# Attention in seven key chunks over two pairs at once, its division moved into the w_in stage, and the row sums of two quads in one phase

## The chip, the cores and the metric

The kernel runs on one core of one Trainium2 chip. The metric is the device time of one execution, in microseconds (us). The kernel before takes 799.59 us, the median of three runs (799.35 to 800.0).

## The reference, cut to what matters

Attention over 8 batches of 12 heads, 448 tokens, head size 64, with q and k normalised row by row, and behind it a feed-forward block on the 3584 x 768 result (inner width 1024). All of it is in float32.

```python
q_n, k_n = rmsnorm(q, g_q), rmsnorm(k, g_k)            # x / sqrt(mean(x*x) + 1e-6) * g
scores = q_n @ k_n.T / sqrt(64)
attn = exp(scores - max) ; attn = attn / (sum(attn) + 1e-9)
x = (attn @ v) laid out as (B*S, H*D)                  # 3584 x 768
h = x @ w_in                                           # 768 x 1024
solu = h * softmax(h)
ln = (solu - mean) / sqrt(var + 1e-6) * g_ln
out = ln @ w_out                                       # 1024 x 768
```

## The kernel before, in words

`fast_path` has three stages, one behind the other: attention, the product with w_in (with the activation and the layer norm of each token tile behind it), and the product with w_out. The order of all instructions is written out by hand: `unit(f)` emits one piece of TensorE work and then whatever was put down to be due, `later(n, f)` puts f down for n units later, and `follow(parts, i, f)` emits f right behind part i. Each engine, and each engine's DMA queue, works in the order of emission and waits at an instruction whose inputs are not there.

**Attention.** The work goes by quads, 24 of them, `for m in range(NQ)` (L1432): a quad is four heads, as two pairs a = 2m and b = 2m + 1. q and k are loaded by 8 transfers per quad on SP's queue (`load`, L631), squared on ScalarE (`squares`, L670), summed by row on VectorE (`row_sums`, L676). The two halves of a row's sum lie in neighbouring groups of 32 partitions: GpSimd copies them across in four copies and adds (`fold_sums`, L684). The inverse root is a Ln and an Exp on ScalarE and four small VectorE instructions (`rsqrt_seed` L693, `rsqrt_step` L700); GpSimd multiplies (`normalise`, L709); VectorE transposes in 32 x 32 blocks (`qk_transpose`, L720); ScalarE applies the gain to q (`gain`, L725).

The 448 keys of a pair are cut into three chunks of 128 (`scores`, L810) and a last one of 64, which two pairs share (`scores_last`, L824): seven groups of four 64 x 64 tiles of TensorE in a quad. ScalarE takes the exponential of each group from PSUM, 128 x 896 at a time (`exponentials`, L806). There is no maximum: the scores are bounded by the gains. The product with v is again seven groups of four tiles: `values_last` (L859) and `values_part` (L873) twice, the two parts apart because a row tile has to change its PSUM bank in between (`turn`, L899, a wait through ScalarE). The first scores of the next quad run between the two parts.

The row sums of the exponentials are a product with ones (`sums`, L914), in tiles of 128 rows by 32 columns. It takes four terms: the shared chunk, one chunk of pair b, and for each pair a tile that VectorE has added up (`add`, L842); GpSimd adds the third chunk of pair a to its tile (`add_more`, L853). Each quad has its own phase of these products at its end. Then the sums are turned, inverted and spread to all rows of the output (`inverse`, L936: a VectorE transpose, a reciprocal, four GpSimd copies; `divide`, L952: a VectorE transpose and the multiplication of the PSUM output, 128 x 896), and the result goes to DRAM by two transfers on SP's queue (`store_x`, L961). The next quad's first values wait for `divide`, since there is one output tile in PSUM.

Beside this, w_in is loaded and converted from float64 in 12 steps (`convert_w`, L518: two ScalarE and two VectorE instructions a step), at the quads of `steps_at` (L1376), and GpSimd forms the combinations of its blocks (`combine_in`, L565).

**w_in.** Seven products instead of eight per block of 256 tokens, 14 blocks g. `load_x(g)` (L974) brings x back from DRAM, for g >= 2 on ScalarE's queue. `sizes` (L985) is two ScalarE instructions, `block_sums` (L1005) four GpSimd ones. `products` (L1019) gives seven parts p1 to p7, each six matmul instructions; `in_parts` (L1149) sets their order, for block g: p6, p5, p7, p1 of g + 1, p4, p2 of g + 1, p3. Behind the parts of block g stand `sizes(g + 1)` and the two halves of `block_sums(g + 1)`, and at the fifth of them `load_x(g + 2)`. The activation and the layer norm of each token tile follow by `later` (`ff_max` to `ff_spread`, L1099 to L1147): on VectorE the sum of two partial products (L1053), the product h * exp (L1112), two statistics (L1120), a transpose (L1141). w_out is loaded and converted beside it.

**w_out.** The same scheme on quarter blocks. The change does not touch it.

Of the kernel before, what the change touches and what calls it, by code (L numbers as in the profile page):

```python
# [366 lines left out]
def fast_path(  # L367
# [29 lines left out]
    NB = S // 32  # L397
    NP = H // 2
# [26 lines left out]
    ones = consts.tile([P, 3, 32], FP32, name="ones")  # L425

    w_in = {k: wi.tile([P, HD, DFF // 2], FP32, name=f"w_in{k}") for k in (0, 5, 1, 4, 3, 6, 2)}
    xd = [dram.tile([DM, S], FP32, name=f"xd{b}") for b in range(B)]
    ud = [dram.tile([2, 4, 32, HF * P], FP32, name=f"ud{t}") for t in range(NT)]
# [88 lines left out]
    def convert_w(step, raw):  # L518
# [15 lines left out]
        def low_bits():  # L534
            nc.scalar.activation(low, lo, AF.Relu, scale=-(2.0 ** -29), bias=seven)
            nc.scalar.activation(tmp[:, 1].bitcast(I32), low, AF.Copy, scale=-1.0, bias=7.0)
# [93 lines left out]

    def load(m):  # L631
        qk = loads.tile([P, 2, 2, NB * 32], FP32, tag="qk", name="qk", bufs=4)
        for s, src in enumerate((q, k)):
            rows = heads(src, m).rearrange("(h i) (b t) (x d) -> h x t (i b) d", h=2, t=32, x=2)
            for g in range(4):
                nc.sync.dma_start(  # L636
                    qk[g * 32 : g * 32 + 32, s].rearrange("p i (b d) -> p (i b) d", d=32), rows[g // 2, g % 2]
                )
        for i in range(2):
            st[2 * m + i] = {"qk": qk[:, :, i]}  # L640

    def load_v(m, queue=nc.sync):


        d = quads[m] = {}
        d["v"] = loads.tile([P, 4, NJ, D], FP32, tag="v", name="v", bufs=2)
        queue.dma_start(
            d["v"].rearrange("p h j d -> p h (j d)"),
            heads(v, m)[:, 0 : NJ * P].rearrange("h (p j) d -> p h (j d)", j=NJ),
        )  # L650
        if m % 2 == 0:
            vl = loads.tile([P, 4, D], FP32, tag="vl", name="vl", bufs=2)
            two = heads(v, m, 8)[:, NJ * P : S].rearrange("(h i) p d -> i p h d", i=2)
            for i in range(2):
                nc.sync.dma_start(vl[i * D : (i + 1) * D], two[i])
                lasts[m + i] = vl[:, 2 * i : 2 * i + 2]
        d["vl"] = lasts.pop(m)
# [15 lines left out]

    def row_sums(n):  # L676
        m, i = divmod(n, 2)
        if i == 0:
            norms[m] = {"part": small.tile([P, 2, 2 * NB], FP32, tag="part", name="part", bufs=2)}
# [159 lines left out]
    def on_vector(m):  # L839
        return m >= NQ - 2  # L840
# [911 lines left out]
```

## Time and profile before

| | |
|---|---|
| time, median of 3 runs | 799.59 us |
| span of the profiled execution | 798.0 us |
| attention, from the start to its last row sums | 311.4 us |
| w_in stage | from 311.7 us to about 565 us |
| w_out stage | from there to the end |
| TensorE busy over the span | 99% |
| VectorE, ScalarE, GpSimd busy | 76%, 59%, 66% |

The profiled execution's own time is its span, 798.0 us from the first to the last instruction; the timed runs are 1.6 us above it, which is what lies around the span. A timeline line gives the start, the duration (of a merged run of like instructions, from the first start to the last end), the engine, the line of the kernel, the operation, output<-input with shapes, and in brackets the idle time of the engine before it and what ended that. Each float32 product stands in the profile as two matmul instructions, so a group of four tiles is eight. "PEld" is the weight load, which runs beside the products. A busy TensorE is not a TensorE at its peak.

### The profile page before, as it was taken

The page shows a single profiled execution, that of the slowest core. Times are in us where ns is not written, and L with a number is a line of the kernel's source. Part 1 is how long each engine was busy: PE and PEld are TensorE (multiplying, and loading weights), DVE is VectorE, ACT ScalarE, POOL GpSimd, SP SyncE. Part 2 cuts the span into 40 slices and gives each one's busy share as a digit, 9 for nine tenths or more (in the row PEclk, how much of TensorE's full clock was granted, in tenths as well). Part 3 has the DMA queues.
Part 4 walks back from the last instruction along what each step waited for, and adds up shares of the span by engine and source line. Part 5 has one row for each costly group of instructions (what it writes and reads, how often), then busy time and mean ns, then how long its engine had stood idle before and what let it go on. Part 6 is the DMA issues. An engine that isn't in the chain of part 4 may idle for free.

```text
span 798.0 us, 15285 instructions
## 1 busy us (share of the span) xinstructions
PE 786.3 (99%) x5382; PEld 468.8 (59%) x5382; DVE 608.7 (76%) x1153; ACT 472.5 (59%) x783; POOL 524.2 (66%) x665
## 2 busy tenths in 40 slices
PE   8999999999999999999999999999999999999997
PEld 4344444444444444444444444444799999999996
DVE  6787989989888895587777667776896776866945
ACT  6777988878779763566766544454515455464410
POOL 2666777778877775243466466668787777877861
PEclk9999999999999999999999999999999999999999
DMA  8878799898787742455545445542757547366312
GB/s 166 162 181 166 165 198 187 198 189 164 166 164 175 152 109 74 132 137 147 152 132 145 106 110 143 140 122 53 207 151 235 176 168 262 127 210 229 108 60 84
DMA packets 266913, 122.74 MB, mean 154 GB/s; under 512 B 184012, under 2 KB 251980, under 8 KB 266828
## 3 DMA queue, kind: packets, MB, share of 16 engines
q1 hardware_dynamic: 252988, 111.78, 56.0%
q10 hardware_dynamic: 13840, 9.90, 4.4%
q8 instruction: 44, 0.72, 0.4%
q14 instruction: 41, 0.34, 0.1%
HBM read 84.94 MB, written 36.70 MB: 152 GB/s over the span
## 4 chain that ended last, share of the span: by engine, by line
PE 86%; DVE 5%; SPq 2%; DMA 2%; issue 1%; ACT 1%; POOL 1%; DVEq 0%; ACTq 0%; POOLq 0%
PE A L1252 14%; PE s L818 13%; PE o L882 12%; PE BD L1037 11%; PE A L1037 11%; PE B L1252 7%; PE sm L931 5%; PE C L1037 5%; PE C L1252 3%; PE o L868 2%; PE s L831 2%; SPq L636 1%; DMA ur<-ud 1%; DVE ub L1141 1%; PE o L909 1%
## 5 line engine op out<-in xcount | busy, mean ns | idle before, releaser
L808 ACT ACTIVATE E<-s 128x896 f32<-128x896 f32 x168 | 141.2, 932 | 11.4 <-PE s L818 11.2
L818 PE MATMUL s<-qkT 64*64 64x448 f32 x1152 | 124.2, 544 | 1.4 <-ACT qkT L792 0.6
L882 PE MATMUL o<-E,v 64*64 64x448 f32 x1056 | 107.1, 536 | 0.0
L1126 POOL TENSOR_TENSOR he<-he,mhalf 128x1 f32<-128x1 f32 x28 | 27.3, 975 | 103.3 <-DVE he L1125 102.8
L818 PEld LDWEIGHTS s<-qkT 64*64 64x64 f32 x1152 | 49.8, 163 | 58.3 <-ACT E L808 25.0
L857 POOL TENSOR_TENSOR es<-es,E 128x896 f32<-128x896 f32 x23 | 49.1, 2133 | 49.4 <-DVE es L845 49.4
L1252 PE MATMUL A<-w_out,sums 128*128 128x192 f32 x392 | 80.0, 327 | 1.2 <-DVE u L1266 1.2
L713 POOL TENSOR_TENSOR qkn<-qk,ny 128x896 f32<-128x896 f32 x46 | 77.9, 1713 | 3.7 <-DVE ny L707 1.5
L1252 PE MATMUL B<-w_out,sums 128*128 128x192 f32 x392 | 79.8, 326 | 0.4 <-DVE P L1314 0.4
L1037 PE MATMUL A<-w_in,xg 128*128 128x512 f32 x168 | 74.6, 593 | 0.0
L882 PEld LDWEIGHTS o<-E,v 64*64 64x64 f32 x1056 | 40.2, 133 | 58.3 <-issue 58.1
L1108 ACT ACTIVATE u<-h,hmax 128x1024 f32<-128x1024 f32 x28 | 32.2, 1148 | 66.4 <-DVE hmax L1102 66.4
L1037 PE MATMUL BD<-w_in,xsum 128*128 128x512 f32 x156 | 71.2, 592 | 0.0
L1252 PEld LDWEIGHTS A<-w_out,sums 128*128 128x128 f32 x392 | 66.1, 190 | 2.3 <-issue 1.4
L1252 PEld LDWEIGHTS B<-w_out,sums 128*128 128x128 f32 x392 | 66.2, 190 | 0.8 <-DVE P L1314 0.7
L845 DVE TENSOR_TENSOR es<-E 128x896 f32<-128x896 f32 x48 | 57.2, 1195 | 0.0
L1037 PEld LDWEIGHTS A<-w_in,xg 128*128 128x128 f32 x168 | 31.8, 190 | 40.1 <-issue 39.3
L723 DVE STREAM_TRANSPOSE qkT<-qkn 128x896 f32<-128x896 f32 x46 | 50.9, 1106 | 4.4 <-POOL qkn L713 4.4
L1037 PEld LDWEIGHTS BD<-w_in,xsum 128*128 128x128 f32 x156 | 29.5, 190 | 37.5 <-issue 35.4
L690 POOL COPY ss<-part 32x56 f32<-32x56 f32 x92 | 46.3, 503 | 6.5 <-DVE part L680 2.2
L680 DVE TENSOR_REDUCE part<-sq 128x28 f32<-128x896 f32 x46 | 47.7, 1077 | 0.8 <-ACT sq L672 0.8
L1252 PE MATMUL A<-w_out,s 128*128 128x192 f32 x224 | 45.6, 326 | 0.3 <-ACT u L1264 0.3
(160 smaller groups left out, 1662.6 us busy)
## 6 DMA issues: line engine op xcount, KB each, us to landing
ur<-ud SPq DMA_DIRECT2D x60, 256.0 KB, 4.7
ud<-ub SPq DMA_DIRECT2D x112, 128.0 KB, 2.3
xd<-xo SPq DMA_DIRECT2D x48, 224.0 KB, 3.0
qk<-in_q_dram SPq DMA_DIRECT2D x92, 112.0 KB, 3.1
qk<-in_k_dram SPq DMA_DIRECT2D x92, 112.0 KB, 3.1
v<-in_v_dram SPq DMA_DIRECT2D x24, 384.0 KB, 4.7
out_dram<-P SPq DMA_DIRECT2D x19, 384.0 KB, 3.7
raw<-in_moe_w_in_dram SPq DMA_DIRECT2D x12, 512.0 KB, 5.0
```

Source lines behind the costliest of these rows:

```text
L680: nc.vector.tensor_reduce(norms[m]["part"][:, i], st[n]["sq"], AX, OP.add)
L690: e.tensor_copy(ss[g * 32 : g * 32 + 32], part[o * 32 : o * 32 + 32])
L713: e.tensor_tensor(d["qkn"].rearrange("p (s b) d -> p s b d", s=2), d["qk"].rearrange("p s (b d) -> p s b d", d=32), y.rearrange("p (s b) - ...
L723: nc.vector.transpose(d["qkT"].rearrange("p s t -> p (s t)"), d["qkn"].rearrange("p b d -> p (b d)"))
L808: nc.scalar.activation(d["E", kc], s[:, :, 0:S], AF.Exp)
L818: nc.tensor.matmul(s[c : c + D, h, 0:S], d["qkT"][hh, 1, keys], d["qkT"][hh, 0, :], start=True, stop=True,)
L845: nc.vector.tensor_tensor(d["es"], d["E", 0], d["E", 1], OP.add)
L857: e.tensor_tensor(d["es"], d["es"], d["E", 2], OP.add)
L882: x = nc.tensor.matmul(d["o"][h * D : (h + 1) * D, :], quads[m]["v"][pp, i + 2 * h, kc], d["E", kc][pp, h], start=False, stop=(part == 1 a ...
L931: nc.tensor.matmul(sm[g : g + 32, :], ones[:, w], e[:, h, t * S // 2 : (t + 1) * S // 2], start=(x == 0), stop=(x == len(terms) - 1),)
L1037: nc.tensor.matmul(k[bank], a[:, c], w_in[i][:, c], start=begin and c == 0, stop=c == HD - 1, skip_group_check=not begin,)
L1252: nc.tensor.matmul(k[bank], a[:, c].rearrange("p a i -> p (a i)"), w_out[:, area, i, c], start=begin and c == 0, stop=c == KC - 1, skip_gr ...
```

## The change

- **Chunks.** Both pairs of a quad go side by side through seven chunks of 64 keys (`both_scores`, `both_values`), each one group of four tiles. Keys are taken with a stride of 7. The parts, the turn and the early scores of the next quad are gone. The gain is one instruction for both pairs. v is loaded by two transfers of 64 partitions. Quad 0 keeps its chunks, with its values at its end.
- **Sums.** VectorE adds chunks 0, 1 and 2 into one tile for both pairs, and 3 and 4 into a second; chunks 5 and 6 are terms of their own: four terms. In quads from 6 on that hold no conversion step (7, 10, 13, 16, 19, 22, 23) chunk 3 joins the first tile and 4 and 5 the second: three terms. GpSimd adds none. The sums of two quads (1 and 2, 3 and 4, to 21 and 22) are one phase of TensorE, behind the even quad; those of quads 0 and 23 stand alone.
- **Division.** The output of a quad is copied undivided from PSUM (`take`, VectorE) and stored. The sums are copied by ScalarE and go to DRAM (`keep_sums`); for each batch one load, one reciprocal of 128 x 42 and one store give the inverses (`load_sums`, `invert`, `send_inverses`). In the w_in stage `load_r(g)` brings the inverses of a block, spread over 64 partitions a head, as a tile as large as x, by four to six transfers on SP's queue; three VectorE multiplications of 128 x 512 (`scale`, parts 0 to 2) stand behind p6, p5 and p7 of the block before, and `sizes` and `block_sums` move back by two parts. Block 0 is scaled in the last quad.
- **Norms.** The halves of the row sums change places by four transfers on SP's queue (`swap_sums`) and one GpSimd addition (`add_swapped`). Squares run two to three quads ahead. q and k come by single pieces, two ahead of the swap and six behind it.
- The conversion steps and the combinations of w_in are spread over other quads.

```diff
+    def both_scores(m, kc):
+        s = ps_t.tile([P, 2, 512], FP32, tag="t", name="s")
+        qkT = quads[m]["qkT"]
+        keys = slice(kc, NK * (D - 1) + kc + 1, NK)
+        for i in range(2):
+            for h in range(2):
+                hh = slice(h * D, (h + 1) * D)
+                nc.tensor.matmul(
+                    s[i * D : (i + 1) * D, h, 0:S], qkT[hh, i, 1, keys], qkT[hh, i, 0], start=True, stop=True
+                )
+        exponentials(quads[m], kc, s, kc == NK - 1)
...
+                nc.tensor.matmul(
+                    d["o"][h * D : (h + 1) * D, i, 0:S], d["v"][pp, h, kc], d["E", kc][pp, h],
+                    start=kc == 0, stop=kc == NK - 1,
+                )
...
+    def swap_sums(m):
...
+        for g in range(2):
+            for a in range(2):
+                nc.sync.dma_start(to[a, g], of[a, 1 - g])
+    def add_swapped(m):
+        d = norms[m]
+        nc.gpsimd.tensor_tensor(d["ss"], d["ss"], d["part"].rearrange("p i b -> p (i b)"), OP.add)
...
+    def sums(ms):
+        sm = ps_t.tile([P, 2, 512], FP32, tag="t", name="sm")
+        for j, m in enumerate(ms):
...
+    def keep_sums(ms, sm):
...
+        nc.scalar.copy(r[:, 0:n], sm[:, 0:n, 0 : S // 2])
+        def send():
+            nc.sync.dma_start(sd[ms[0] : ms[0] + n].rearrange("j r c -> r j c"), r[0:P:16, 0:n])
...
+    def take(m):
...
+        nc.vector.tensor_copy(d["xo"], d["o"][:, :, 0:S])
...
-        nc.vector.transpose(r, d["rc"].rearrange("p i t b -> p (i t b) ()").to_broadcast([P, 2 * NB, 32]))
-        nc.vector.tensor_tensor(xo, d["o"][:, :, 0:S], r.rearrange("d (i b) x -> d i (b x)", i=2), OP.mult)
...
+    def load_r(g):
...
+                    nc.sync.dma_start(
+                        x[h * D : (h + 1) * D, :, o : o + k], r.rearrange("c t -> () c t").to_broadcast([D, w, k])
+                    )
...
+        for c, r in parts:
+            nc.vector.tensor_tensor(x[:, c], x[:, c], r, OP.mult)
...
-                follow(parts, x, lambda g=g: sizes(g + 1))
-                follow(parts, x + 1, lambda g=g: block_sums(g + 1, 0))
-                follow(parts, x + 2, lambda g=g: block_sums(g + 1, 1))
+                for i in range(3):
+                    follow(parts, x + i, lambda g=g, i=i: scale(g + 1, i))
+                follow(parts, x + 2, lambda g=g: sizes(g + 1))
+                follow(parts, x + 3, lambda g=g: block_sums(g + 1, 0))
+                follow(parts, x + 4, lambda g=g: block_sums(g + 1, 1))
             if g + 2 < NG:
-                follow(parts, x + 4, lambda g=g: load_x(g + 2))
+                follow(parts, x + 4, lambda g=g: (load_x(g + 2), load_r(g + 2)))
...
+    EARLY = 6
+    steps_at = (5, 6, 8, 9, 11, 12, 14, 15, 17, 18, 20, 21)
+    inverts_at = {5: (0,), 9: (1,), 11: (2,), 15: (3,), 17: (4,), 21: (5,), 23: (6,)}
```

The order of a quad from 6 on, as the new loop emits it (quads 2 to 5 differ in the squares and row sums, which stand between the first scores; quad 1 has an order of its own, with the row sums of quad 3 and `fold_sums` in it):

```python
            if sent: keep_sums                       # ScalarE, behind an even quad
            load_v(m + 1); take(m - 1); store_x(m - 1); sent()
            rsqrt_step(norms[m + 1]); normalise(a + 2); normalise(b + 2)
            combine_in(x); invert(x); load_pieces(2)
            row_sums(a + 4); row_sums(b + 4); swap_sums(m + 2); load_pieces(6)
            score(0); score(1); qk_transpose(a + 2); qk_transpose(b + 2)
            score(2); add_swapped(m + 2); score(3); value(0); score(4); low_bits[0]()
            value(1); score(5); low_bits[1](); gains(m + 1)
            add_pair(m, 0, 1); add_to(m, 0, 2, nc.vector); add_pair(m, 3, 4)
            value(2); score(6); join(); rsqrt_seed(norms[m + 2])
            squares(a + 6); squares(b + 6); load_next()
            value(3) ... value(6); sums of this quad and the one before, if m is even
```

568 lines of the change are left out of this document (328 added, 240 removed).

## The prediction

> **What bounds the kernel now.** I read the page first (totals, the chain that ended last), then the stretches by window, then the timeline of one quad and of one block of the w_in stage, and last the groups of VectorE, GpSimd and SP's queue.
>
> ```profile
> span 798.0 us, 15285 instructions
> PE 786.3 (99%) x5382; PEld 468.8 (59%) x5382; DVE 608.7 (76%) x1153; ACT 472.5 (59%) x783; POOL 524.2 (66%) x665
> PE 86%; DVE 5%; SPq 2%; DMA 2%; issue 1%; ACT 1%; POOL 1%; DVEq 0%; ACTq 0%; POOLq 0%
> ```
>
> TensorE is busy nearly throughout and makes up 86% of the chain. So time can go only where TensorE's own work goes, and it comes back wherever another engine makes TensorE wait. Stretches: one quad, and two blocks of the w_in stage (with and without conversion of w_out beside it).
>
> ```profile
> core 0: us, PE busy (x) PEld busy (x) DVE busy (x) ACT busy (x) POOL busy (x), PEclk, DMA share, GB/s
> 187.36:199.72 12.36, 12.36 (x148) 5.44 (x144) 11.31 (x17) 9.95 (x15) 9.93 (x14) 1.00 0.91 188
> 383.70:401.70 18.00, 18.00 (x43) 7.98 (x42) 15.23 (x32) 12.41 (x21) 8.63 (x11) 1.00 0.68 176
> 455.70:473.70 18.00, 18.00 (x44) 7.96 (x43) 11.98 (x26) 8.25 (x14) 10.54 (x13) 1.00 0.39 103
> ```
>
> TensorE has no gap in any of them; VectorE is next, with 1.05 us free in a quad, 2.8 and 6.0 us in a block. The clock is full. One quad on TensorE:
>
> ```profile
> 224.65 0.96 PE L931 MATMUL sm<-E,ones 128*32 128x224 f32 x16
> 225.43 0.94 PE L931 MATMUL sm<-es,ones 128*32 128x224 f32 x16
> ...
> 227.89 0.93 PE L831 MATMUL s<-qkT 64*64 64x448 f32 x8
> 228.64 2.43 PE L818 MATMUL s<-qkT 64*64 64x448 f32 x24
> ...
> 237.02 0.96 PE L931 MATMUL sm<-E,ones 128*32 128x224 f32 x16
> ```
>
> A group of four tiles (eight instructions) takes 227.89 to 228.64, 0.75 us; 14 of them are 10.50. The quad takes 237.02 - 224.65 = 12.37. Of the other 1.87, the sums' 32 instructions at 0.78 per 16 are 1.56; 0.31 us is left, the price of going into the 128 x 32 tiles and out again.
>
> **The change, part by part: TensorE.** Scores and values stay at 14 groups a quad. Phases of sums: 24 before; after, quads 0 and 23 alone and 11 double ones, 13. That removes 11 x 0.31 = 3.41 us. A term is eight instructions, 0.39 us: seven quads lose one (2.73), quad 0 gains one (its chunks of pair b go in unadded: 0.39). Together 5.75 us, as long as nothing becomes late.
>
> **The first quads.** Before, the start is not clean either:
>
> ```profile
> 23.68 0.96 PE L931 MATMUL sm<-E,ones 128*32 128x224 f32 x16
> 38.72 0.96 PE L931 MATMUL sm<-E,ones 128*32 128x224 f32 x16
> L808 ACT ACTIVATE E<-s 128x896 f32<-128x896 f32 x168 | 141.2, 932 | 11.4 <-PE s L818 11.2
> 227.38 4.97 ACT L808 ACTIVATE E<-s 128x896 f32<-128x896 f32 x6 [0.82 <-PE s L818]
> L680 DVE TENSOR_REDUCE part<-sq 128x28 f32<-128x896 f32 x46 | 47.7, 1077 | 0.8 <-ACT sq L672 0.8
> L723 DVE STREAM_TRANSPOSE qkT<-qkn 128x896 f32<-128x896 f32 x46 | 50.9, 1106 | 4.4 <-POOL qkn L713 4.4
> L845 DVE TENSOR_TENSOR es<-E 128x896 f32<-128x896 f32 x48 | 57.2, 1195 | 0.0
> L690 POOL COPY ss<-part 32x56 f32<-32x56 f32 x92 | 46.3, 503 | 6.5 <-DVE part L680 2.2
> L697 ACT ACTIVATE ny<-ss,eps 128x56 f32<-128x56 f32 x19 | 6.5, 342 | 39.5 <-POOL ss L691 39.5
> L672 ACT ACTIVATE sq<-qk 128x896 f32<-128x896 f32 x38 | 34.7, 988 | 0.0
> ```
>
> Quad 1 takes 15.04 us there, 12.37 plus an early score group 0.75 would be 13.12: 1.9 lost. After the change, quad 1's scores start near 25.8 (the last gain of quad 0's loop ends about then). Exponentials stand 0.81 apart ((4.97 - 0.93) / 5). After the copy of the sums (estimate 0.6), three of them and the seed (0.34 and about 0.25) ScalarE is at 30.1. VectorE then has the step of the root (four small ones, estimate 0.8), two adds, a transpose, row sums, a transpose: 2.4 + 2.2 + 1.1, to 36.6; the gain of 896 elements (a Square of that size is 0.99) ends at 37.5, and only then can quad 2 score. TensorE would be through at 25.8 + 10.5 = 36.3: 1.2 lost. The second row sums and the fold (four copies of 0.5 and an addition) end near 40, the seed at 40.6; quad 2's first exponential stands behind it, and its fourth score group waits for that PSUM buffer: 41.5 against 39.8, at most 1.7 lost, 0.9 if the fold is quicker. Then two squares stand between quad 2's exponentials, 0.3 to 0.7 more. I take 3.0 us (2.0 to 4.0); against 1.9 before, 1.1 more. The free end is no loss at all, 1.9 gained.
>
> **The steady quad, costed at nothing, with its cover.** Per pair of quads TensorE will need 2 x 10.5 + 3.12 + 0.31, 12.2 a quad.
> VectorE:
>
> ```profile
> 201.71 0.42 DVE L942 STREAM_TRANSPOSE r<-sm 128x224 f32<-128x224 f32 x1 [1.45 <-PE sm L931]
> 202.16 0.33 DVE L943 RECIPROCAL rc<-r 128x28 f32<-128x28 f32 x1
> 203.53 1.11 DVE L956 STREAM_TRANSPOSE r<-rc 128x896 f32<-128x896 f32 x1 [0.15 <-POOL rc L950]
> 204.68 1.09 DVE L957 TENSOR_TENSOR xo<-o,r 128x896 f32<-128x896 f32 x1
> ```
>
> It loses these four (2.95) and gains the plain copy from PSUM (nearest, the last row: 1.09) and one more add (1.2): 11.31 - 2.95 + 1.09 + 1.2 = 10.65 of 12.2; in a quad of three terms one more add takes the place of the conversion. If that cover went, each us over 12.2 would be paid in each quad. The copy stands at the quad's start; the first values wait for it, but four score groups (3.0 us) run first, so up to 1.9 us of backlog are hidden. ScalarE loses one fixed cost of two gains and gains half a copy: about 10. Its order (exponential 4, conversion, 5, conversion, gains, 6) brings exponential 6 out near 9.6 us into the quad; the last value group wants it at 9.8: close, no loss taken, 0.3 in each of 12 quads at worst. GpSimd drops from 9.9 to about 5.
>
> SP's queue. Before:
>
> ```profile
> 175.72 0.49 SPq L647 DMA_DIRECT2D v<-in_v_dram  x1
> 181.06 1.25 SPq L966 DMA_DIRECT2D xd<-xo  x2
> 182.42 3.10 SPq L636 DMA_DIRECT2D qk<-in_q_dram  x4
> 185.56 3.37 SPq L636 DMA_DIRECT2D qk<-in_k_dram  x4
> ...
> 58.42 3.84 SPq L636 DMA_DIRECT2D qk<-in_q_dram  x4
> ```
>
> After: eight pieces 6.5, the store 1.25, v in two (shaped like the store: 1.25), the swap's four (no such row; 0.49 to 0.81 each by these, I take the store's 0.62: 2.5), w_in and sums about 0.8: 12.3, just the length of a quad. The swap waits for the second row sums (about 4 us into an even quad), with six pieces queued behind it and the next store behind those; GpSimd's addition and the seed wait for it, with about 3 us to spare. Loads run over a quad ahead. I take nothing lost; the bound is a rival below.
>
> **The w_in stage.** VectorE gains three products of 128 x 512 in each of 13 blocks.
>
> ```profile
> L1213 DVE TENSOR_TENSOR s<-ur x14: 693/948/1201, 508.4 to 739.4; 128x512 f32<-128x512 f32 x14
> 422.28 0.40 ACTq L982 DMA_DIRECT2D xg<-xd  x1
> 465.49 1.22 DVE L1112 TENSOR_TENSOR u<-h,u 128x1024 f32<-128x1024 f32 x1
> 466.75 1.29 DVE L1120 BATCH_NORM_STATS2 bs<-u 128x6 f32<-128x512 f32 x2
> 467.20 5.31 PE L1037 MATMUL A<-w_in,xg 128*128 128x512 f32 x12
> 470.60 0.69 DVE L1053 CUSTOM_DVE_ANT_0 h<-BD,u 128x512 f32<-128x512 f32 x1 [1.18 <-ACT u L1044]
> xg<-xd ACTq DMA_DIRECT2D x7, 768.0 KB, 5.3
> ```
>
> Three times 0.69 to 1.20 is 2.1 to 3.6 us a block, against 2.8 free in the tightest and 6.0 in a quiet one. The path is short: p1 of the next block needs its first two chunks from scale 0 and the third from scale 1. In the quiet block scale 0 would stand at 466.7, the statistics and their small followers after it, scale 1 at 469.5 to 470.2; p1 (the second half of the 12) starts near 469.8 and wants its third chunk 1.7 later, 471.5. Covered by 1.3, and the sum at 470.60 is barely moved. In the six or so blocks with conversion, its two VectorE instructions or a backlog eat that. I take 0.25 us in each of those six, 1.5 in all; ends 0 and 6 x 1.8. The inverses are as large as x (5.3 us): from the load of x at 422.28 to that block's scale 0, some 9.4 us later, both fit if they share the transfers' time, barely if one is after the other.
>
> **Sum.** -5.75 + 1.1 + 1.5 = -3.15: span 794.9, and as the median lies 1.6 above the span, 796.4 us.
>
> [...]
>
> ```profile
> 197.20 2.11 POOL L857 TENSOR_TENSOR es<-es,E 128x896 f32<-128x896 f32 x1 [1.39 <-DVE es L845]
> 198.68 1.58 DVE L845 TENSOR_TENSOR es<-E 128x896 f32<-128x896 f32 x1
> ```
>
> This add starts 0.63 before GpSimd's product ends and takes 1.58, 0.39 over the mean of all, 1.195. [...]
>
> **Rivals.**
> 1. *The gain comes whole* (start no worse than before, scales hidden): 799.6 - 5.75 = 793.9, 792.0 if the start is clean. For it: TensorE's own sum. Against: the chain at quad 2.
> 2. *The scales are partly late*: 3 to 6 us lost in w_in, 798 to 801, no change. For it: VectorE at 15.23 + 2.1 to 3.6 of 18.
> 3. *Slower: VectorE in w_in.* In the six blocks with conversion scale 1 stands behind statistics and conversion and reaches p1 1.8 us late, 10.8 in all: -5.75 + 1.1 + 10.8, 805.7. It decides where three scales cost over 2.8 us a block. Against: 6 us free in the others.
> 4. *Slower: SP's queue.* If a piece takes 0.96 (3.84 for four, the costliest row) instead of 0.81 (6.5 / 8), the queue needs 13.5 a quad, late by 1.3 in each of 13 quads until the swap's 3 us are gone: +14, 810. Before, transfers of q reach that only in the busiest quad; now fewer w_in loads fall together.
> [...]
>
> **How the numbers follow.** Chances: forecast 0.52, rival 1 0.13, rival 2 0.15, rivals 3, 4, 5 0.10, 0.07, 0.03. Faster by over 0.2% (1.6 us, about what a measurement of this kernel tells from no change): 0.52 + 0.13 = 0.65; same 0.15; slower 0.20. The range runs from 792.5, inside rival 1, to 803.0, short of the full rivals 3 to 5: about 2 in 10 are left out.
>
> **What would show it.** Right: quads with a phase 13.9 us and those without 10.5; 13 phases; TensorE without idle time from quad 3 on, attention's end near 307; about 3 us of waits around quads 1 and 2, ended by the gain and an exponential; w_in's length within 2 us of before. Wrong: p1's third chunk or the sums of partial products waiting on VectorE in each block; the seed of the root waiting for GpSimd's addition each quad; the conversion waiting for its load; the first values waiting for the copy from PSUM.

## The result and the profile after

The changed kernel takes 847.43 us (median; 844.11 to 853.43), against 799.59 before: 1.0607 times as long, 95% interval 1.056 to 1.0653. A fourth run of the kernel before took 890.6 us, 11% above the other three, and is left out of its median. The forecast of 796.4 had the wrong sign, and the time lies far outside its range. The page of the changed kernel, whose profiled execution took 853.43 us, 6 us above the median:

```profile
span 851.6 us, 15237 instructions
PE 796.3 (94%) x5374; PEld 480.0 (56%) x5374; DVE 620.5 (73%) x1157; ACT 476.6 (56%) x774; POOL 432.0 (51%) x466
PE 52%; DVE 15%; DMA 12%; SPq 10%; issue 5%; ACT 3%; POOL 2%; DVEq 0%; ACTq 0%; POOLq 0%
```

TensorE made up 86% of the chain that ended last and now makes up 52%. DMA and the issues of SP's queue (SPq), 4% together before, are 22%; GpSimd is busy 92 us less. To see where, I divide both spans at the first matmul of w_in and the first of w_out that reads the tile `sums` (the very first of w_out stands some 1.9 us earlier, in every kernel here). The stretches of the kernel after, then w_in before:

```profile
53.00:344.80 291.80, 263.53 (x2974) 122.04 (x2970) 215.14 (x282) 207.90 (x285) 97.10 (x76) 0.99 0.80 155
344.80:621.60 276.80, 262.26 (x604) 114.67 (x601) 200.21 (x422) 137.49 (x226) 152.93 (x159) 0.98 0.66 153
621.60:851.60 230.00, 222.94 (x1364) 220.79 (x1362) 166.24 (x394) 96.68 (x212) 162.75 (x192) 0.99 0.51 169
```
```profile
311.70:567.00 255.30, 255.01 (x604) 113.43 (x601) 180.77 (x386) 137.05 (x225) 144.05 (x165) 1.00 0.47 125
```

The columns are those of the windows in the prediction: length, busy time of PE, PEld, DVE, ACT and POOL, clock, DMA share, GB/s. Attention ends at 344.8 us instead of 311.7 (+33.1), w_in takes 276.8 instead of 255.3 (+21.5), the rest 230.0 instead of 231.0. There are two losses to explain. In w_in TensorE is idle for 14.5 us (0.3 before), and the same 604 matmuls take 7.3 us more of busy time. What TensorE waits for, in attention from 53 us on, and in w_in:

```profile
PE o L906 <- ACT El L854: 13.4, 10, 2.9
PE s L894 <- ACT E L854: 7.6, 6, 5.0
PE s L894 <- ACT gcol L480: 3.0, 1, 3.0
```
```profile
PE A L1115 <- DVE xg L1063: 7.9, 5, 4.2
PE BD L1115 <- DVE top L1131: 6.4, 2, 4.2
```

Before the change the same view of attention is empty. The releasers are late exponentials on ScalarE, and in w_in VectorE's products and sums. An engine named here is only the last link, though. One quad of the timeline, SP's queue first:

```profile
211.66 0.54 SPq L513 DMA_DIRECT2D raw<-in_moe_w_in_dram  x1
212.33 1.37 SPq L673 DMA_DIRECT2D v<-in_v_dram  x2
213.81 1.60 SPq L1010 DMA_DIRECT2D xd<-xo  x2
215.51 1.61 SPq L644 DMA_DIRECT2D qk<-in_q_dram  x2
217.22 4.35 SPq L699 DMA_DIRECT2D ss<-part  x4
221.62 1.17 SPq L644 DMA_DIRECT2D qk<-in_q_dram  x2
222.83 3.58 SPq L644 DMA_DIRECT2D qk<-in_k_dram  x4
226.45 0.76 SPq L513 DMA_DIRECT2D raw<-in_moe_w_in_dram  x1
```
```profile
218.33 0.76 ACT L538 ACTIVATE tmp<-raw,seven 128x512 f32<-128x512 uint32 x1 [2.87 <-DMA raw<-in_moe_w_in_dram]
221.24 0.91 ACT L854 ACTIVATE El<-s 128x896 f32<-128x896 f32 x1
223.33 0.34 ACT L728 ACTIVATE ny<-ss,eps 128x56 f32<-128x56 f32 x1 [1.18 <-POOL ss L703]
```
```profile
222.20 0.98 PE L906 MATMUL o<-El,v 64*64 64x448 f32 x8 [1.27 <-ACT El L854]
```

From 211.66 to 226.45 SP issues with no gap above 0.13 us. The swap's four issues take 4.35 us of it, where four at their median of 0.59 would take 2.4; what stretches them the profile doesn't say. From one raw block to the next are 14.8 us, where TensorE's work is 12.2. The raw block of w_in issued at 211.66 comes too late for the conversion at 218.33, two exponentials of ScalarE stand behind that, and at 222.20 TensorE waits for the second. The seed (L728) waits for the swapped sums as well. Which of the two matters is what the experiments had to tell.

### The profile page after: what moved, and what is told of

Same layout as the page of the kernel before. It is cut to its first block, busy times and chain, and to the rows that moved or that the text cites. A ratio compares the mean times of both kernels' runs of the same rounds, so it can differ in the third digit from the quotient of the medians.

```text
span 851.6 us, 15237 instructions
## 1 busy us (share of the span) xinstructions
PE 796.3 (94%) x5374; PEld 480.0 (56%) x5374; DVE 620.5 (73%) x1157; ACT 476.6 (56%) x774; POOL 432.0 (51%) x466
## 4 chain that ended last, share of the span: by engine, by line
PE 52%; DVE 15%; DMA 12%; SPq 10%; issue 5%; ACT 3%; POOL 2%; DVEq 0%; ACTq 0%; POOLq 0%
PE A L1332 13%; PE BD L1115 8%; PE A L1115 7%; PE B L1332 7%; SPq L644 5%; DMA xg<-xd 4%; PE C L1332 3%; PE s L894 3%; PE o L906 3%; SPq L699 3%; PE C L1115 2%; DMA inv<-sd 2%; DVE qkT L765 2%; DVE part L711 2%; POOL qkn L744 2%
## 5 line engine op out<-in xcount | busy, mean ns | idle before, releaser
L894 PE MATMUL s<-qkT 64*64 64x448 f32 x1288 | 144.3, 552 | 14.8 <-ACT E L854 8.7
L854 ACT ACTIVATE E<-s 128x896 f32<-128x896 f32 x144 | 124.4, 919 | 18.7 <-PE s L894 17.8
L906 PE MATMUL o<-E,v 64*64 64x448 f32 x1104 | 122.1, 541 | 1.8 <-ACT E L854 1.8
L894 PEld LDWEIGHTS s<-qkT 64*64 64x64 f32 x1288 | 64.7, 192 | 80.2 <-issue 42.4
L1115 PE MATMUL A<-w_in,xg 128*128 128x512 f32 x168 | 77.4, 603 | 8.1 <-DVE xg L1063 7.9
L1204 POOL TENSOR_TENSOR he<-he,mhalf 128x1 f32<-128x1 f32 x28 | 31.2, 1114 | 86.4 <-DVE he L1203 86.1
L703 POOL TENSOR_TENSOR ss<-ss,part 128x56 f32<-128x56 f32 x20 | 8.2, 409 | 129.8 <-DMA ss<-part 125.9
L914 DVE TENSOR_TENSOR es<-E 128x896 f32<-128x896 f32 x46 | 52.0, 1130 | 1.5 <-ACT E L854 1.5
L1115 PEld LDWEIGHTS BD<-w_in,xsum 128*128 128x128 f32 x156 | 29.4, 190 | 37.5 <-issue 34.0
L1210 ACT ACTIVATE u<-u,shift,he 128x1024 f32<-128x1024 f32 x28 | 34.7, 1241 | 27.0 <-POOL shift L1206 27.0
L1115 PE MATMUL BD<-w_in,xg 128*128 128x512 f32 x84 | 42.7, 648 | 6.4 <-DVE top L1131 6.4
```

Source lines behind the costliest of these rows:

```text
L854: nc.scalar.activation(e, s[:, :, 0:S], AF.Exp)
L894: nc.tensor.matmul(s[i * D : (i + 1) * D, h, 0:S], qkT[hh, i, 1, keys], qkT[hh, i, 0], start=True, stop=True)
L906: nc.tensor.matmul(d["o"][h * D : (h + 1) * D, i, 0:S], d["v"][pp, h, kc], d["E", kc][pp, h], start=kc == 0, stop=kc == NK - 1,)
L914: nc.vector.tensor_tensor(e, d["E", x], d["E", y], OP.add)
L1115: nc.tensor.matmul(k[bank], a[:, c], w_in[i][:, c], start=begin and c == 0, stop=c == HD - 1, skip_group_check=not begin,)
L1210: nc.scalar.activation(d["u"], d["u"], AF.Identity, scale=d["e"], bias=d["shift"])
```

## The experiments

Each time below is a median of four runs (of three for the kernel before); the ratio is to the kernel before as it ran beside each one (medians of 799.0 to 799.3 us in those runs), with its interval. The stage lengths come from one profiled execution each. "Attention" is the time at which it ends.

| kernel | attention | w_in | time | ratio |
|---|---|---|---|---|
| before | 311.7 | 255.3 | 799.59 | |
| after | 344.8 | 276.8 | 847.43 | 1.0607 (1.056 to 1.0653) |
| swap_undone | 310.7 | 271.2 | 816.04 | 1.0228 (1.0189 to 1.0268) |
| invert_late | 339.7 | 279.5 | 850.06 | 1.0616 (1.0585 to 1.0647) |
| both_attention | 315.7 | 273.8 | 819.89 | 1.0232 (1.019 to 1.0273) |
| swap_first | 348.2 | 276.6 | 852.67 | 1.0647 (1.0606 to 1.0688) |
| swap_unused | 341.1 | 279.1 | 854.04 | 1.0708 (1.0671 to 1.0744) |
| swap_no_wait | 336.6 | 272.6 | 844.02 | 1.0567 (1.0549 to 1.0584) |
| swap_half | 317.2 | 270.3 | 823.33 | 1.0319 (1.0289 to 1.0349) |
| swap_gpsimd | 316.9 | 272.8 | 822.12 | 1.0293 (1.0262 to 1.0324) |
| v_scalar | 357.4 | 275.2 | 865.85 | 1.0836 (1.0806 to 1.0865) |
| one_r_load | 344.1 | 257.6 | 834.69 | 1.0428 (1.0391 to 1.0466) |
| fold_r_scalar | 311.1 | 279.4 | 823.46 | 1.0303 (1.0286 to 1.032) |
| fold_r_gpsimd | 311.8 | 279.5 | 824.13 | 1.0307 (1.0284 to 1.0331) |
| fold_r_early | 310.7 | 273.6 | 813.83 | 1.018 (1.0163 to 1.0197) |
| x_gpsimd | 310.8 | 270.4 | 814.26 | 1.0192 (1.0175 to 1.0209) |
| raw_three | 311.7 | 279.2 | 822.17 | 1.028 (1.0263 to 1.0297) |
| r_one_transfer | 310.6 | 265.3 | 810.66 | 1.0149 (1.013 to 1.0168) |
| r_quarter | 310.6 | 260.3 | 803.48 | 1.0061 (1.0044 to 1.0077) |
| r_no_products | 312.2 | 269.0 | 2361.16 | see its text |

The first ten kernels after the one before (after to v_scalar) have the same code in w_in, and their w_in took 270.3 to 279.5 us. So much scatter has that stage, and only what lies outside it counts below.

### Attention: the swap, undone

```diff
-                    swap_sums(m + 2)
...
-                    add_swapped(m + 2)
+                    fold_sums(m + 2)
```

> The swap of the row sums by four DMAs is taken back: GpSimd folds the sums with four copies and an addition, as before the change, at the place where it added the swapped ones. All else is as after the change. Theory S (the swap is what makes attention late: SP's queue, the landing, GpSimd's addition, the seed ahead of the next squares and exponentials on ScalarE): attention, which ends at 344.8 us, ends at 315 to 320, the seed's waits for GpSimd (36.7 us in 17) all but vanish, and the time falls from 847.4 to some 820. Rival I (VectorE waits for the load of the inverses, 23 us in four waits, and hands its lateness on): at most 10 us fall away, 838 or more, and the four waits stay. Rival E (exponentials of the last chunk come late by ScalarE's own order of work): attention stays within 5 us of 344.8.

```diff
-                for x in inverts_at.get(m, ()):
-                    invert(x)
...
                     join()
+                for x in inverts_at.get(m, ()):
+                    invert(x)
+                    send_inverses(x)
```

> The swap stays; in the seven quads that invert a batch's row sums the reciprocal and the store of its result move from the quad's beginning on VectorE and SP to its end, behind the adds and the join. Theory S (the swap): attention falls by 5 to 10 us, the share of the quads in which swap and inverses fell together, and most of the seed's waits stay; about 840. Rival I (inverses): the four waits of VectorE (23 us) go, and attention ends near 322; about 825.

> Both at once: the fold on GpSimd in place of the swap, and the reciprocal at the quad's end. If swap and inverses together make the loss of attention, it ends at 307 to 312 (the prediction on record has 307) and the time is 810 to 815. If ScalarE's own order of work is at fault (rival E), attention ends above 330 still. If the two cost separate amounts, the gain of this kernel is the sum of the gains of the two kernels that undo one each; if they cost the same stalls, it is clearly less than the sum.

With the fold attention ends at 310.7, 34.1 us earlier, even below the 315 to 320 of theory S. The swap it is, then; whether by the seed, as theory S also says, is still open. The late inverses do nothing that the times can tell: alone they take 850.06 us, with the fold 819.89, where 810 to 815 was expected. Rival I falls, although VectorE stood 23 us for them. TensorE's waits with the fold, from 53 us on, and its row by windows:

```profile
PE sm L966 <- DVE es L914: 1.1, 1, 1.1
PE o L906 <- ACT El L854: 0.5, 1, 0.5
PE s L894 <- ACT r L977: 0.2, 1, 0.2
```
```profile
53.00:310.70 257.70, 255.88 (x2978) 123.84 (x2970) 213.20 (x278) 206.96 (x283) 142.94 (x151) 1.00 0.88 172
```

Idle time is 1.8 us instead of 28.3, and busy time for the same matmuls 255.9 instead of 263.5. Together these are the 34 us; of the second part some 2.7 us are the clock, by the estimate at the end. GpSimd does 46 us more work than after, and TensorE's waits don't name it.

### Attention: the way of the row sums, or the queue

I then believed in a closed circle: the seed lets GpSimd multiply, this frees the buffer of the next two pieces, the swap stands behind these in SP's queue, and the next seed stands behind the swap. Two kernels against it, one that puts the swap ahead of the pieces and one whose swapped sums nobody reads:

```diff
-                    load_pieces(2)
...
                     swap_sums(m + 2)
-                    load_pieces(6)
+                    load_pieces(8)
```

> The swap stays as the change made it, with its four DMAs, their landing and GpSimd's addition; only its place in SP's queue changes: from the sixth quad on it stands ahead of all eight pieces of q and k, not behind the first two. Those two wait for GpSimd's multiplications of the quad, which free their buffer, and by the trace these end 1.5 us after the row sums. Theory C (a closed circle: seed, step, GpSimd's multiplications, the two pieces that wait for them on SP, the swap behind these, the addition, the next seed; some 14 us around, where a quad of TensorE's work is 12.2): with the swap ahead of the pieces the circle is cut, attention ends at 312 to 322 instead of 344.8, the time falls to 815 to 826. Rival D (the swap's own length, 2.5 us of issue and about 1.5 us of landing between row sums and seed, is what makes the seed late wherever it stands): attention stays above 332.

```diff
-        to = d["ss"].rearrange("(a g p) x -> a g p x", a=2, g=2)
+        to = work.tile([P, 4 * NB], FP32, tag="sx", name="sx", bufs=2).rearrange("(a g p) x -> a g p x", a=2, g=2)
...
-                    add_swapped(m + 2)
+                    fold_sums(m + 2)
```

> GpSimd folds the row sums as before the change, and the four DMAs of the swap still run at their old place in SP's queue, into a tile that nobody reads. Theory C (the seed is late because it stands behind the queue): attention is as with the fold alone, which ended at 310.7, or a few us later: 311 to 318. Rival Q (the four DMAs cost by holding up SP's queue, so that pieces, stores and w_in's loads come late, whoever reads the swapped sums): attention ends above 328.

The circle is refuted twice. With the swap ahead attention ends no earlier (348.2). With the unused swap it ends at 341.1, though the seed waits for GpSimd 12.6 us in 8 quads instead of 36.7 in 17. The four DMAs cost nearly all of the loss whoever reads what they bring: rival Q. Three kernels say how:

```diff
-        of = d["part"].rearrange("(a g p) i b -> a g p (i b)", a=2, g=2)
+        of = ident[:, 0 : 4 * NB].rearrange("(a g p) x -> a g p x", a=2, g=2)
```

> GpSimd folds the row sums, and the four small DMAs stay at the swap's place in SP's queue, but they copy a constant into a tile that nobody reads, so they wait for no engine. The kernel with the unused swap, whose DMAs do wait for VectorE's row sums, ended attention at 341.1 us; the fold alone at 310.7. Theory W (SP's queue stands still while the swap at its head waits for the row sums): attention ends at 311 to 318. Theory I (four more issues of 0.62 us, or four more transfers among those that may be under way at once, fill the queue): it stays above 330.

```diff
-        for g in range(2):
+        for g in range(1):
```

> As the kernel with the unused swap, but two of its four DMAs are left out: GpSimd folds, and two transfers that nobody reads wait for the row sums at the swap's place. Theory W (the wait at the head of the queue, whatever stands behind it): little changes, above 332. Theory I (the number of issues): the queue needs 1.2 us a quad less, and attention ends about half way, 320 to 330, or all the way down where the queue is just full with four.

```diff
-                nc.sync.dma_start(to[a, g], of[a, 1 - g])
+                nc.gpsimd.dma_start(to[a, g], of[a, 1 - g])
```

> The swap is used as the change made it (GpSimd adds what the four DMAs bring, the seed waits for it), but GpSimd issues the four DMAs, so SP's queue holds none of them. Theories W and I alike (SP's queue): attention ends at 311 to 320. Theory T (the transfers themselves, or the way of the row sums through DMA to the seed): it stays above 330.

None, two and four unused DMAs a quad end attention at 310.7, 317.2 and 341.1; four that wait for no engine at 336.6. So the number of DMAs on SP's queue decides, and the wait for the row sums at its head is the small part: 4.5 us in these two profiles, and the spread of single runs may account for part of that. Issued by GpSimd, the swap in full use leaves attention at 316.9. What ScalarE's seed waits for there, and TensorE from 53 us on:

```profile
ACT ny L728 <- POOL ss L703: 31.1, 16, 4.0
```
```profile
PE s L894 <- ACT E L854: 2.6, 5, 1.4
PE sm L966 <- DVE es L914: 1.1, 1, 1.1
PE s L894 <- ACT r L977: 1.0, 1, 1.0
```

The seed still waits 31.1 us in 16 quads, and TensorE hardly notices. That wait, which I took for the cause, is covered in this kernel, and it stood in the profile of before already, larger, with TensorE waiting for nothing. Its line before and after:

```profile
ACT ny L697 <- POOL ss L691: 46.1, 23, 3.3
```
```profile
ACT ny L728 <- POOL ss L703: 36.7, 17, 6.6
```

Added up over the timeline's rows from 118 to 310 us, SP's issues take 118.0 us before (171 of them), 138.9 with the fold, 138.9 with GpSimd's issues, 155.8 with two unused, 165.3 with four that don't wait, 166.7 with four that do, and 170.3 after (240). From the fold on the end of attention rises in that order. The sum alone doesn't set it: the swap issued by GpSimd ends attention 6.2 us after the fold at the same 138.9, and by the same count swap_first has 162.4 us and ends at 348.2. In these 192 us the kernel after does 13.5 quads (27 stores), 12.6 us of issues in each quad and 14.2 us a quad; the rest is waits in order. The last kernel of this row moves two issues a quad to ScalarE:

```diff
-                load_v(m + 1)
...
                 score(0)
+                if next1:
+                    load_v(m + 1, nc.scalar)
```

> As after the change, swap and all, but the two transfers of the next quad's values are issued by ScalarE behind the quad's first exponential instead of by SP at its start. SP's queue has two issues less in a quad (1.37 us) and no longer stands at its head for the values' buffer; the number of transfers and their bytes are the same. Theory I (what is full is SP itself, by issue times and by its waits in order): attention falls from 344.8 to 310 to 325 us. Theory F (what is full is the number of transfers under way, eight): it stays above 332.

This made it worse, 357.4, with only 146.2 us of issues on SP from 118 to 310. It lies where theory F had it, but doesn't tell the two theories apart, because it brought a wait of its own. SP's waits in it, from 53 us on:

```profile
SPq L1010 <- DMA v<-in_v_dram: 23.0, 8, 6.5
SPq L980 <- DMA v<-in_v_dram: 12.5, 3, 4.5
```

The trace shows why a store waits for a load that has nothing to do with it. The 792 issues of SP (771) and ScalarE (21) in the trace of the kernel after name eight semaphores, 99 each. The program gives them out in turn, and an issue waits until the transfer that had this semaphore before has landed: on the one semaphore whose landings that trace has in full, none of the 98 later issues starts before that landing; before the change, on four such semaphores, none of 307. The waits in the program's order (after the change, the swap of one quad and what follows):

```
168 L699 DMA ss_1495<-part_1492 32x56 [waits DMAHW4_49,DVE_49]
169 L699 DMA ss_1495<-part_1492 32x56 [waits DMAHW5_49]
...
173 L644 DMA qk_1489<-in_q_dram 32x28x32 [waits DMAHW1_49]
174 L644 DMA qk_1489<-in_k_dram 32x28x32 [waits DMAHW2_49]
```

So every further DMA costs SP its issue (0.59 us at the median of the swap's) and a place among the eight. GpSimd's issues are in neither count: with four of them a quad SP's sum is 138.9 us, as with the fold, and with x issued by GpSimd (below) SP's 33.5 us of waits for x are gone. How much of the swap's price is the one and how much the other stays open. The trace of the kernel after speaks for the issues and the waits in order: from 118 to 310 us it puts 2.3 us of SP's waits down to landings and 26.5 us to other engines, where in v_scalar it puts 39.4 us down to landings. But issues that are stretched, as the one at 217.22, may hide such a wait.

### w_in: the loads of the inverses

```diff
-            tiles = [sums_in.tile([P, KD * 2 * P], FP32, tag="r", name="rg", bufs=1)]
+            tiles = kept_r or [sums_in.tile([P, KD * 2 * P], FP32, tag="r", name="rg", bufs=1)]
+            held = bool(kept_r)
+            kept_r[:] = tiles
...
-        for i, x in enumerate(gs[g, "r"]):
+        for i, x in enumerate(gs[g, "r"] if not g or not held else ()):
```

> Attention is as after the change. In the w_in stage the inverses spread over the partitions are loaded for blocks 0 and 1 alone, and block 1's stay in place for all later blocks: their products are made with the wrong inverses, which leaves the loads of twelve blocks out and all of VectorE's products in. Theory L (these loads and what stands behind them on SP's queue make w_in late: the stage's 21.6 us more): w_in falls from 274.9 us to 253 to 258 and the time from 847.4 to some 829. Rival V (VectorE's three products a block): w_in stays at 268 or more, the time at 840 or more.

w_in falls to 257.6, 2.3 above before, with all of VectorE's products in it: theory L. (The 274.9 in the expectation counts up to the very first matmul of w_out; by that boundary it is 255.7 now. The time fell less than expected, to 834.69.) In its waits of TensorE hardly anything is left:

```profile
PE BD L1119 <- DVE top L1135: 1.3, 1, 1.3
PE A L1119 <- DVE xg L1067: 0.9, 2, 0.5
```

All kernels from here on have the fold. First, other queues, another time, another buffer:

```diff
-                    nc.sync.dma_start(
+                    (nc.sync if g < 2 else nc.scalar).dma_start(
                         x[h * D : (h + 1) * D, :, o : o + k], ...
```

> The fold in place of the swap, and from block 2 on the loads of the spread inverses are issued by ScalarE, behind its load of x, instead of by SP: same transfers, same bytes. Beside the fold alone (816.0 us; w_in from its first matmul to w_out's first 271.2 us, where before the change it was 255.3). Theory H (in SP's queue these loads stand ahead of the stores of u and of the loads of w_out, and what they wait for holds these up): w_in falls to 257 to 262, the time to 802 to 807. Rival B (the bytes: the inverses slow every other transfer): w_in stays within 3 us of 271. Rival A (ScalarE pays for the issues instead, some 2.5 us a block, and copies its sums of partial products late): w_in is longer than 271.

> As the kernel that moves the loads of the spread inverses to ScalarE, but GpSimd issues them. Theory H (SP's queue): w_in falls from 271.2 to 257 to 262 us, the time to 802 to 807. Rival B (the bytes): it stays within 3 us of 271. Between the two queues: if ScalarE's kernel is slower than this one, ScalarE's own work behind the issues is the difference; GpSimd has 8 to 10 of 18 us a block free.

```diff
+                follow(parts, x + 3, lambda g=g: load_r(g + 2))
-                follow(parts, x + 4, lambda g=g: (load_x(g + 2), load_r(g + 2)))
+                follow(parts, x + 4, lambda g=g: load_x(g + 2))
```

> The fold in place of the swap, and in w_in the load of a block's spread inverses is issued one part (3.6 us) earlier, a part ahead of the load of x instead of together with it; all is still issued by SP. With the fold alone w_in took 271.2 us. Theory L (the two loads of 768 KB come together and late, and what waits for them, VectorE's product, the store of u and w_out's loads behind them on SP, holds TensorE up): w_in falls to 258 to 265 us and the time to 803 to 810. Rival B (the bytes cost wherever they stand): w_in stays within 3 us of 271.

```diff
-            (nc.sync if g < 2 else nc.scalar).dma_start(x[:, :, o : o + n], ...
+            (nc.sync if g < 2 else nc.gpsimd).dma_start(x[:, :, o : o + n], ...
```

> The fold in place of the swap; the load of a block's x is issued by GpSimd from block 2 on, so it is none of the eight transfers that SP's and ScalarE's queues may have under way, and no store of u can wait for it. Theory N: SP's waits for x (33.5 us in the stage) vanish and w_in falls by at least half of its excess, to 256 to 264. Theory B, or theory V (VectorE stands at its product until x and inverses have landed, whatever SP does): w_in stays at 268 or more, and longer than 272 if GpSimd comes late to the issue.

```diff
-            raw = conv.tile([P, HO, 2], U32, tag="raw", name="raw", bufs=2)
+            raw = conv.tile([P, HO, 2], U32, tag="raw", name="raw", bufs=3)
...
-        for _ in range(2):
+        for _ in range(3):
             load_next()
```

> The fold in place of the swap; in w_in three buffers instead of two hold the raw w_out, so each of its loads is issued a conversion earlier. If late raw w_out (ScalarE's conversion stands for it, its copies of partial sums and VectorE's sums behind it) is how the loads of the inverses reach TensorE, w_in falls below 264 us, from 271.2 with the fold alone. If the way is another (stores of u late, VectorE's products late), w_in stays within its scatter, 268 to 275.

All five stay within the scatter. The earlier loads don't even remove the wait that they were aimed at: SP still stands 33.8 us for x. Two others remove all or most of theirs, and TensorE waits all the same. With the fold alone SP stands for the load of x, which holds one of the eight semaphores; with x issued by GpSimd that line is gone, yet TensorE waits at VectorE's product:

```profile
SPq L1222 <- DMA xg<-xd: 33.5, 12, 5.7
```
```profile
PE A L1115 <- DVE xg L1063: 9.5, 9, 1.7
PE BD L1115 <- DVE top L1131: 2.5, 3, 1.3
```

With three raw buffers ScalarE's wait for w_out falls from 6.4 to 2.0 us, and TensorE again waits at the product, more than before. So theories H (SP's order), L (together and late) and the late raw buffer are refuted as the one carrier. Then the transfers themselves, half as many with the same bytes, and as many with a quarter of the bytes:

```diff
-                for h in range(2):
...
-                    r = r[h, half, i * w : (i + 1) * w, c : c + k]
+                r = r[0, half, i * w : (i + 1) * w, c : c + k]
...
+                nc.sync.dma_start(x[:, :, o : o + k], r.rearrange("c t -> () c t").to_broadcast([P, w, k]))
```

> The fold in place of the swap (attention at 310.7, w_in 271.2 us). In w_in one transfer brings the inverses of the even heads to all 128 partitions, where two brought each half its own: half the transfers (26 instead of 52), the same bytes; the odd heads are multiplied by the wrong inverses. Theory N (number: eight transfers may be under way, each further one waits for the eighth before it, and the four for the inverses bring the stores of u up against the load of x): w_in falls to 258 to 264. Theory B (bytes): w_in stays above 268.

```diff
+        n = 16 if g and held else D
...
-                        x[h * D : (h + 1) * D, :, o : o + k], r.rearrange("c t -> () c t").to_broadcast([D, w, k])
+                        x[h * D : h * D + n, :, o : o + k], r.rearrange("c t -> () c t").to_broadcast([n, w, k])
```

> The fold in place of the swap; the same number of transfers for the inverses as after the change, at the same places, but from block 2 on each writes 16 partitions instead of 64, a quarter of the bytes (the other rows keep block 1's inverses, which are wrong there). Theory B (bytes: x and its inverses together land late): w_in falls to 257 to 262. Theory N (number): w_in stays above 266.

```diff
-                for i in range(3):
-                    follow(parts, x + i, lambda g=g, i=i: scale(g + 1, i))
```

> The fold in place of the swap; all loads of the inverses stay, but from block 1 on VectorE's products with them are left out, so x goes in undivided. Theory V (VectorE's wait at the product, in order ahead of its other work, or the products' 2.1 us a block): w_in falls to 254 to 259. Theories N and B (the loads hold up SP's stores of u and w_out's loads, which ScalarE and VectorE wait for): w_in stays above 264.

A quarter of the bytes brings w_in to 260.3, half the transfers to 265.3. Both lie below the scatter. The first is what theory B had said (a quarter of the bytes also means fewer packets, 52513 in the stage instead of 66288, so the two aren't told apart). For the second B had said above 268 and N at most 264; it lies between, so number counts too, for less. The time is 810.66 us with one transfer and 816.04 with two halves. Without the products w_in stays at 269.0: VectorE's part is small, or at least no larger than the scatter. (Undivided x exceeds the kernel's bound for its fast path, so the second path runs behind it; hence 2361 us, and only the stage is read.) The windows of w_in with a quarter of the bytes, and with the loads of blocks 0 and 1 alone:

```profile
310.60:570.90 260.30, 256.08 (x605) 113.22 (x602) 201.97 (x422) 137.13 (x226) 154.04 (x159) 1.00 0.56 135
```
```profile
344.10:601.70 257.60, 255.37 (x604) 113.23 (x601) 202.42 (x422) 137.03 (x226) 154.56 (x159) 1.00 0.51 127
```

The DMA share goes from 0.47 before to 0.51, 0.56 and 0.66 after. By which engine the fuller transfers reach TensorE changes from kernel to kernel, and isn't settled.

## Why the prediction was wrong, point by point

- **TensorE's own sum held in the steady quads.** With the fold the phases of sums start at 148.92, 172.97 and 197.43: two quads take 24.05 us with seven terms and 24.46 with eight, where the working has 24.04 and 24.43. The start came as worked out too: after the change quad 2 scores from 37.5 us, and the first double phase ends at 53.05. Still, attention ends at 310.7 with the fold, where the working gives 307. Nearly all of the 3.7 us lie in four places, with the waits listed above among them: the pairs of quads that begin at 50.01, 74.97 and 221.48 take 0.5, 1.0 and 0.6 us longer than that, and the last double phase 1.3. Of the 4.7 us that attention was to gain (5.75 less 1.1), 1.0 came.
- **The failed step: SP's queue, "just the length of a quad ... I take nothing lost".** The sum was right (12.3 forecast, 12.6 measured), in part by luck: the pieces took 5.1 us a quad instead of 6.5, the swap 3.6 instead of 2.5. What I made of it was wrong. This queue also waits, in order, for GpSimd, VectorE and TensorE (all engines together 26.5 us from 118 to 310 us), so with 12.6 us of issues a quad took 14.2 and not 12.2. Before, its issues took 118.0 of 192 us. I put the loss at nothing; against the fold it is 34.1 us. Rival 4 had 14: it named the place, but its condition didn't come (a piece took 0.68 us on average, not 0.96), its price was too small, and 0.07 far too unlikely. The queue decides earlier than I wrote: two DMAs more already end attention 6.5 us later.
- **"About 3 us to spare" for the seed.** The seed waits in 17 quads, but that isn't the main cost, as the kernels with the unused swap and with GpSimd's issues show. My list of wrong signs named this wait and the conversion that waits for its load, and both came. Both reach TensorE at times: the second in the quad shown above, the first some three microseconds before it, where ScalarE stands 2.03 us for the swapped sums, then takes the seed and two squares, and TensorE waits 1.15 us for the exponential behind them:
```profile
208.76 0.34 ACT L728 ACTIVATE ny<-ss,eps 128x56 f32<-128x56 f32 x1 [2.03 <-POOL ss L703]
210.98 3.32 ACT L854 ACTIVATE E<-s 128x896 f32<-128x896 f32 x4
211.93 1.04 PE L894 MATMUL s<-qkT 64*64 64x448 f32 x8 [1.15 <-ACT E L854]
```

- **The inverses, "both fit if they share the transfers' time".** This is the second failed step. I priced VectorE in w_in and let the loads go with a comparison of lengths. They cost nearly all of the 21.5 us: with those of twelve blocks left out, 2.3 are left. Bytes carry most of it and the number of transfers some; by which engine they reach TensorE stays open.
- **VectorE's products**: 1.5 us taken; they cost at most the 2.3 us that w_in has more than before when the loads are out. Rival 3 (10.8) did not happen.
- **Adds beside GpSimd's work.** In both traces the adds that overlap an instruction of GpSimd are longer: before, 33 of them take 1.259 us on average and the other 15 1.054; after, 17 take 1.233 and 29 take 1.069. No run shows the loss that the chances hold at 0.03 as rival 5: the mean of all these adds fell from 1.195 us to 1.130.

```profile
L914 DVE TENSOR_TENSOR es<-E 128x896 f32<-128x896 f32 x46 | 52.0, 1130 | 1.5 <-ACT E L854 1.5
```

No kernel here beats the one before. The best that leaves nothing out, fold_r_early, takes 813.83 us. Even with both losses out, these figures leave next to no gain: attention is 1.0 us shorter with the fold, and w_in 2.3 us longer with the loads out.

## What to carry to other kernels

Add up the issues of each DMA queue for a period of the kernel, whatever the transfers' size (0.59 us for 7 KB and 0.58 for 112 KB here), and take a queue that would be busy all of the period (here 12.6 us of issues for 12.2 of TensorE's work) as the new bound, not as one that just fits; then ask which transfers share a limited set of semaphores (eight here). A long wait (the seed's 36.7 us) is no proof: take its consumer away and see whether the time moves. The division put off to a later stage was paid there by bringing the divisors back, as large as the data: nearly all of the 21.5 us.

## What the hardware showed that I had not expected

A transfer of 7 KB took SP as much time to issue (0.59 us at the median) as one of 112 KB (0.58). The issues of the swap after and of the pieces of q before, min, median and max in ns:

```profile
L699 SPq DMA_DIRECT2D ss<-part x80: 508/590/2767, 49.3 to 311.7; - x80
```
```profile
L636 SPq DMA_DIRECT2D qk<-in_q_dram x92: 312/578/2347, 4.4 to 271.1; - x92
```

The queue that issues them made a large difference: the same four DMAs issued by GpSimd made attention 27.9 us shorter (316.9 against 344.8). How much of it is SP's time and how much the semaphores shared with ScalarE is open, as said above.

TensorE also lost its clock after three of its stops. After 5.03 us without work the same eight matmuls take 1.78 us, and 0.92 again 5.7 us later:

```profile
102.72 1.78 PE L894 MATMUL s<-qkT 64*64 64x448 f32 x8 [5.03 <-ACT E L854]
104.28 1.71 PE L906 MATMUL o<-E,v 64*64 64x448 f32 x8
108.46 0.92 PE L894 MATMUL s<-qkT 64*64 64x448 f32 x8
```
The granted clock is 0.50 in this stretch of the kernel after, and in two more of its w_in stage:

```profile
101.30:108.10 6.80, 5.38 (x32) 1.87 (x36) 6.03 (x6) 4.45 (x6) 3.12 (x2) 0.50 0.67 168
459.70:466.50 6.80, 5.86 (x7) 2.52 (x8) 3.82 (x7) 4.04 (x8) 3.06 (x4) 0.50 0.31 68
575.80:582.60 6.80, 4.92 (x6) 2.19 (x7) 4.10 (x10) 3.51 (x6) 5.25 (x6) 0.50 0.24 48
```

The stops ahead of these stretches lasted 5.03, 4.22 and 4.24 us; after one of 3.02 us at 66 us the clock stayed at 1.00. At half the clock half of the busy time in these windows (5.38, 5.86 and 4.92 us) is lost, by estimate 2.7, 2.9 and 2.5 us. So each of these stalls cost more than itself. In w_in this is 5.4 of the 7.3 us more of busy time, in attention 2.7 of 7.7; where the other 5 us in attention come from, no run here shows.
